# Attention with the scores' keys on the partitions, no transposes of the probabilities, and row sums from a product with ones

## The chip, the core and the metric

The program runs on one core of a Trainium2 chip. A core has TensorE (PE, matrix products), VectorE (DVE), ScalarE (ACT), GpSimd (POOL) and the engine that issues the DMAs here (SP). The metric is the device time of one execution in microseconds (us). All arithmetic is in fp32. A product in fp32 shows in the trace as two MATMUL records.

## The reference

```python
def rmsnorm(x, g):
    return x / np.sqrt(np.mean(x * x, axis=-1, keepdims=True) + 1e-06) * g
q_n, k_n = rmsnorm(q, g_q), rmsnorm(k, g_k)            # (8, 12, 448, 64) each
scores = np.matmul(q_n, k_n.transpose(0, 1, 3, 2)) / np.sqrt(64)
scores = scores - np.max(scores, axis=-1, keepdims=True)
attn = np.exp(scores)
attn = attn / (np.sum(attn, axis=-1, keepdims=True) + 1e-09)
x = np.matmul(attn, v)       # then (8, 12, 448, 64) -> (3584, 768)
r = np.maximum(x @ w_in, 0)  # w_in (768, 2048), float64
out = (r * r) @ w_out        # w_out (2048, 768), float64
```

The gains are g = |randn(64)| + 0.5. The largest product g_q g_k of the inputs used is 5.26.

## The kernel before

There are 8 batches of 12 heads, and attention runs on one pair of heads at a time (2 x 64 = 128 partitions), so there are 6 pairs in a batch and 48 in all. The 448 tokens of a head are split as token = 4 p + j, p on 112 partitions. A unit of work is one j of the queries of a pair, 192 units in all.

For a pair, `norm` (L133 to L148) squares q and k on POOL (L137), sums on DVE (L140), takes the power -1/2 of 112 x 16 numbers on POOL (L141, L142) and multiplies q and k by it on POOL (L144, twice). `transposes` (L150) turns q and k by 8 products with a unit matrix (L157) and moves them out of PSUM on DVE with the gains (L159).

For a unit, `softmax` (L161) makes the scores of 112 queries with 448 keys for both heads (L167: contraction over 64 partitions, head 0 on partitions 0 to 63, head 1 on 64 to 127). DVE takes the row maximum (L170). ACT takes the exponential and sums it (L174, once a head). DVE adds 1e-9, inverts and scales the rows (L177 to L180). `values` (L187) turns the probabilities, 4 products a head (L195), copies them out of PSUM on ACT for head 0 (L198) and on DVE for head 1 (L200), and multiplies them with v, 4 products a head of 112 columns, which write 64 PSUM partitions for each head (L204). After the last unit of a pair DVE copies the result to xT (L209).

`feed_forward` (L217) of a batch is laid in pieces between the units of the next batch. Its first product has 16 groups of 6 products of 448 columns (L224), each followed by a relu on ACT (L227) and a square on POOL (L228). Its second product has 6 groups in an even batch and 8 in an odd one, of 16 products of 384 columns (L236).

During batch 0 there is no feed-forward work. In its place the weights come in as 32 pieces of 768 doubles a partition, and are rounded to fp32: 5 operations on DVE (L110, L112, L113, L115, L116), 2 on ACT (L111, L114), one on POOL (L117), in three sets of buffers that rotate. The feed-forward block of batch 0 starts when all this is done, since the buffers of the raw words lie in its tile gT.

Each engine works through its instructions in one order. A scheduler in the language's layer sets it from the order of the code and from the tiles' buffers: the tag "m" in PSUM (3 buffers before) serves the transposes and both feed-forward products, the tag "s" (2 buffers) the scores, the tag "o" (1 buffer) the product with v.

Of the kernel before, what the change touches and what calls it, by code (L numbers as in the profile page):

```python
# [8 lines left out]
F32 = mybir.dt.float32  # L9
U32 = mybir.dt.uint32  # L10
AF = mybir.ActivationFunctionType
ALU = mybir.AluOpType
AX = mybir.AxisListType.X


@with_exitstack
def kernel(
    ctx: ExitStack,
# [9 lines left out]
):  # L28
    """Softmax attention with RMS-normalised q and k, then relu(x w_in)^2 w_out, all in fp32.

    Attention runs on one pair of heads at a time (2 x 64 = 128 partitions).
    A sequence of 448 tokens is split as token = 4 p + j, with p on 112
    partitions, so that a partition's 4 tokens are one run in memory. A unit of
    work is one j of the queries of one pair: scores and softmax with the
    queries on the partitions, then the normalised rows are transposed and
    multiplied with v, which gives x transposed, as the first product of the
    feed-forward block takes it. The feed-forward block of a batch is laid
    between the units of the next batch.
    """
    nc = tc.nc  # L40

    B, H, S, D = q.shape
    NT, DM = out.shape
    DFF = w_in.shape[1]
    P = 128
# [25 lines left out]

# [1 line left out]
    # Doubles come in pairs of words (low, high) and are rounded here to fp32, the  # L73
    # widest type of the engines: +-2^E from the high word, times
    # 1 + (m20 + low 2^-32) 2^-20. Below fp32's normal range a weight becomes 0,
    # above it infinite. The words stay in gT until the feed-forward block needs it.
    NW = 768
# [40 lines left out]

# [1 line left out]
    qks, vs, qkTs, probs, pavs, xTs = {}, {}, {}, {}, {}, {}  # L120
# [91 lines left out]

# [1 line left out]
    # gT has room for 448 + 64 tokens. An even batch takes the last 448 columns  # L214
    # and leaves its last 64 tokens there for the odd batch that follows, which
    # takes the first 448 and shares its last block of 128 with them.
    def feed_forward(b):  # L217
# [36 lines left out]

# [1 line left out]
    load(0)  # L256
# [15 lines left out]
    for b in range(B):  # L272
        fill = feed_forward(b - 1) if b else iter(())  # starts at its first next()
        n = pieces(b - 1) if b else 0
        done = 0
        for u in range(NPAIR * NJ):
            i, j = b * NPAIR + u // NJ, u % NJ
            if j == 0 and i + 2 < NP:
                load(i + 2)
            softmax(i, j)  # L280
            if j == 1 and i + 1 < NP:
                norm(i + 1)
            if j == 3 and i + 1 < NP:
                transposes(i + 1)
            if last is not None:
                values(*last)
            last = (i, j)
            if b == 0:
                m = len(pieces_w)
                for n_w in range(m * u // (NPAIR * NJ), m * (u + 1) // (NPAIR * NJ)):  # L290
                    round_weights(n_w)
                    load_weights(n_w + NSET)
            while done < n * (u + 1) // (NPAIR * NJ):
                next(fill)
                done += 1
        for _ in fill:
            pass
# [3 lines left out]


# [1 line left out]
_INS = ['q', 'k', 'v', 'g_q', 'g_k', 'moe_w_in', 'moe_w_out']  # L304
# [26 lines left out]
```

## Time and profile before

| | |
|---|---|
| device time, three runs | 2096.97, 2096.86, 2093.71 us; median 2096.86 |
| span of the profiled execution | 2093.7 us |
| PE busy | 1981.1 us (95%) |
| POOL, DVE, ACT busy | 535.5, 838.1, 494.4 us |
| batch 0 of attention with the rounding | 0 to 275 us, DVE busy 235.5 us of it |
| 7 batches of attention with feed-forward | 275 to 1940 us, PE busy 1646.4 us of it |
| last feed-forward block | 1940 to 2089 us |

The profiled execution's own time is its span, with the lowest of the three run times 2093.71 us and the median 3.2 us above it. Busy time of PE is a union of records whose ends are modelled, so a reader goes by starts: how far apart two groups of products begin is what one of them takes.

### The profile page before, as it was taken

The page shows a single profiled execution, that of the slowest core. Times are in us where ns is not written, and L with a number is a line of the kernel's source. Part 1 is how long each engine was busy: PE and PEld are TensorE (multiplying, and loading weights), DVE is VectorE, ACT ScalarE, POOL GpSimd, SP SyncE. Part 2 cuts the span into 40 slices and gives each one's busy share as a digit, 9 for nine tenths or more (in the row PEclk, how much of TensorE's full clock was granted, in tenths as well). Part 3 has the DMA queues.
Part 4 walks back from the last instruction along what each step waited for, and adds up shares of the span by engine and source line. Part 5 has one row for each costly group of instructions (what it writes and reads, how often), then busy time and mean ns, then how long its engine had stood idle before and what let it go on. Part 6 is the DMA issues. An engine that isn't in the chain of part 4 may idle for free.

```text
span 2093.7 us, 22618 instructions
## 1 busy us (share of the span) xinstructions
PE 1981.1 (95%) x9088; PEld 1130.0 (54%) x9088; DVE 838.1 (40%) x1533; ACT 494.4 (24%) x1181; POOL 535.5 (26%) x408
## 2 busy tenths in 40 slices
PE   4767699999999999999999999999999999999999
PEld 2444455555555555555555555555555555555555
DVE  7898853333333333333333333333333333333000
ACT  2344332212221222212221122212222122221100
POOL 4345542311321132311231123221231113210100
PEclk7566599999999999999999999999999999999999
DMA  4233300000000010010000000001000000000000
GB/s 149 93 128 104 123 27 13 28 29 21 23 18 21 29 31 17 14 35 29 14 23 26 29 21 27 14 21 42 14 14 33 31 21 15 17 8 16 0 8 23
DMA packets 47784, 70.67 MB, mean 34 GB/s; under 512 B 3648, under 2 KB 35904, under 8 KB 47680
## 3 DMA queue, kind: packets, MB, share of 16 engines
q1 hardware_dynamic: 47680, 69.22, 10.2%
q8 instruction: 73, 1.20, 0.2%
q14 instruction: 31, 0.25, 0.0%
HBM read 58.20 MB, written 11.01 MB: 33 GB/s over the span
## 4 chain that ended last, share of the span: by engine, by line
PE 81%; DVE 13%; issue 5%; POOL 1%; DMA 0%; SPq 0%; ACT 0%; POOLq 0%; DVEq 0%; ACTq 0%
PE ph L224 29%; PE po L236 25%; PE pav L204 12%; PE sc L167 8%; PE ppt L195 7%; DVE nmax L170 3%; DVE pr L180 1%; DVE qkT L159 1%; DVE w L116 1%; DVE gT L113 1%; DVE gT L112 1%; DVE w L110 1%; DVE rstd L140 1%; DVE w L115 1%; POOL qkn L137 1%
## 5 line engine op out<-in xcount | busy, mean ns | idle before, releaser
L224 PE MATMUL ph<-xT,w 128*128 128x448 f32 x1536 | 626.8, 549 | 1.1 <-DVE xT L209 1.1
L236 PE MATMUL po<-w,gT 128*128 128x384 f32 x1792 | 617.7, 492 | 0.0
L170 DVE TENSOR_REDUCE nmax<-sc 112x2 f32<-112x896 f32 x192 | 209.2, 1090 | 799.2 <-PE sc L167 799.2
L236 PEld LDWEIGHTS po<-w,gT 128*128 128x128 f32 x1792 | 326.7, 190 | 207.8 <-DVE qkT L159 2.8
L224 PEld LDWEIGHTS ph<-xT,w 128*128 128x128 f32 x1536 | 275.0, 190 | 231.2 <-issue 208.0
L204 PEld LDWEIGHTS pav<-prT,vt 112*64 112x64 f32 x3072 | 275.2, 144 | 165.4 <-ACT prT L198 104.3
L204 PE MATMUL pav<-prT,vt 112*64 112x112 f32 x3072 | 334.4, 278 | 6.8 <-DVE prT L200 6.2
L228 POOL TENSOR_TENSOR gT<-r 128x448 f32<-128x448 f32 x128 | 119.4, 933 | 752.7 <-ACT r L227 752.7
L174 ACT ACTIVATE pr<-sc,nmax 112x448 f32<-112x448 f32 x384 | 240.2, 630 | 184.8 <-DVE nmax L170 180.3
L167 PE MATMUL sc<-qkT 64*112 64x448 f32 x768 | 228.9, 626 | 34.0 <-DVE qkT L159 17.5
L195 PE MATMUL ppt<-ident,pr 112*112 112x112 f32 x1536 | 207.8, 277 | 42.6 <-DVE pr L180 23.1
L195 PEld LDWEIGHTS ppt<-ident,pr 112*112 112x112 f32 x1536 | 158.4, 140 | 152.9 <-issue 113.4
L137 POOL TENSOR_TENSOR qkn<-qk 112x1024 f32<-112x1024 f32 x48 | 91.8, 1912 | 533.3 <-issue 380.7
L227 ACT ACTIVATE r<-ph 128x448 f32<-128x448 f32 x128 | 69.6, 544 | 602.5 <-PE ph L224 602.5
L198 ACT COPY prT<-ppt 112x448 f32<-112x448 f32 x192 | 102.1, 532 | 412.6 <-PE ppt L195 412.6
L180 DVE TENSOR_SCALAR pr<-pr,rec 112x448 f32<-112x448 f32 x384 | 174.5, 497 | 5.8
L142 POOL TENSOR_TENSOR rstd<-rstd,mhalf 112x16 f32<-112x16 f32 x48 | 139.6, 2909 | 4.0
L167 PEld LDWEIGHTS sc<-qkT 64*112 64x112 f32 x768 | 61.1, 183 | 147.3 <-issue 105.2
L200 DVE COPY prT<-ppt 112x448 f32<-112x448 f32 x192 | 118.0, 614 | 16.0 <-PE ppt L195 15.9
L144 POOL TENSOR_TENSOR qkn<-qk,rstd 112x512 f32<-112x512 f32 x96 | 107.1, 1136 | 3.8
L241 DVE COPY osb<-po 128x384 f32<-128x384 f32 x28 | 15.6, 558 | 229.0 <-PE po L236 229.0
L117 POOL TENSOR_TENSOR w<-gT,w 128x768 f32<-128x768 f32 x32 | 65.4, 2047 | 112.5 <-DVE w L116 65.3
(27 smaller groups left out, 630.4 us busy)
## 6 DMA issues: line engine op xcount, KB each, us to landing
gT<-in_moe_w_in_dram SPq DMA_DIRECT2D x16, 768.0 KB, 4.5
gT<-in_moe_w_out_dram SPq DMA_DIRECT2D x16, 768.0 KB, 4.2
qk<-in_q_dram SPq DMA_DIRECT2D x48, 224.0 KB, 2.7
qk<-in_k_dram SPq DMA_DIRECT2D x48, 224.0 KB, 2.9
vt<-in_v_dram SPq DMA_DIRECT2D x48, 224.0 KB, 2.5
out_dram<-osb SPq DMA_DIRECT2D x24, 384.0 KB, 2.3
out_dram<-osb SPq DMA_DIRECT2D x8, 192.0 KB, 2.6
gains<-in_g_q_dram SPq DMA_DIRECT2D x2, 0.2 KB, 2.8
```

Of the source, the lines that this page charges most:

```text
L137: nc.gpsimd.tensor_tensor(sq, flat, flat, ALU.mult)
L142: nc.gpsimd.tensor_tensor(rflat, rflat, mhalf, ALU.pow)
L167: nc.tensor.matmul(sc[:, h, 0:S], qkT[rows, 0, j * SP:(j + 1) * SP], qkT[rows, 1, :], start=True, stop=True)
L170: nc.vector.tensor_reduce(nmax, sc[:, :, 0:S], AX, ALU.max, negate=True)
L174: nc.scalar.activation(pr[:, h], sc[:, h, 0:S], AF.Exp, bias=nmax[:, h:h + 1], accum_out=total[:, h:h + 1])
L180: nc.vector.tensor_scalar(pr[:, h], pr[:, h], rec[:, h:h + 1], None, ALU.mult)
L195: nc.tensor.transpose(pt[:, c, :], pr[:, h, c * SP:(c + 1) * SP], ident[:SP, :SP])
L200: nc.vector.tensor_copy(prT, pt)
L204: nc.tensor.matmul(pav[h * D:(h + 1) * D, j * SP:(j + 1) * SP], vt[:, h, c, :], prTs[h][:, c, :], start=(c == 0), stop=(c == NJ - 1))
L224: nc.tensor.matmul(ph, w1[:, c, f * P:(f + 1) * P], xT[:, c, :], start=(c == 0), stop=(c == NPAIR - 1))
L228: nc.gpsimd.tensor_tensor(gT[:, f, c0:c0 + S], r, r, ALU.mult)
L236: nc.tensor.matmul(po, gT[:, f, c0 + t:c0 + t + P], w2[:, f, cols], start=(f == 0), stop=(f == NFC - 1))
```

## The change

The kernel becomes two programs behind a condition that the chip evaluates. The maximum over d of (g_q g_k)^2 is taken on DVE, loaded into a register of each engine and compared with 75^2/64 = 87.9. Up to this bound the program `attention_then_ffn_bounded` runs, above it the kernel before, word for word, as `attention_then_ffn_with_row_max`.

In the bounded program a unit is 112 keys of a pair with all its 448 queries: the scores come with the keys on the partitions, so that their exponential can be multiplied with v as it is. There is no row maximum and no transpose of probabilities. ACT takes one exponential of 112 x 896 a unit. POOL adds the four exponentials of a pair (three additions of 112 x 896). A product of the sum with a 112 x 64 block of ones gives the row sums on all 64 partitions of a head (`finish`, L492). DVE inverts them (128 x 448, L494), and multiplies the product with v by the result as it moves it to xT (L495). The product with v has 448 columns; its heads alternate within each c (L484).

```diff
-    ps_m = ctx.enter_context(tc.tile_pool(name="ps_m", bufs=3, space=bass.MemoryType.PSUM))
+    ps_m = ctx.enter_context(tc.tile_pool(name="ps_m", bufs=2, space=bass.MemoryType.PSUM))
+    ones = consts.tile([SP, D], F32, name="ones")
-        vt = loads.tile([SP, 2, NJ, D], F32, tag="vt", name="vt", bufs=3)
+    def load_v(i):
+        vs[i] = loads.tile([SP, 2, NJ, D], F32, tag="vt", name="vt")
...
-    def softmax(i, j):
+    def scores(i, c):
         qkT = qkTs[i]
         sc = ps_s.tile([SP, 2, 512], F32, tag="s", name="sc")
         for h in range(2):
             rows = slice(h * D, (h + 1) * D)
-            nc.tensor.matmul(sc[:, h, 0:S], qkT[rows, 0, j * SP:(j + 1) * SP], qkT[rows, 1, :],
+            nc.tensor.matmul(sc[:, h, 0:S], qkT[rows, 1, c * SP:(c + 1) * SP], qkT[rows, 0, :],
                              start=True, stop=True)
-        nc.vector.tensor_reduce(nmax, sc[:, :, 0:S], AX, ALU.max, negate=True)
-        pr = work.tile([SP, 2, S], F32, tag="pr", name="pr", bufs=3)
-        for h in range(2):
-            nc.scalar.activation(pr[:, h], sc[:, h, 0:S], AF.Exp, bias=nmax[:, h:h + 1],
-                                 accum_out=total[:, h:h + 1])
-        nc.vector.tensor_scalar(total, total, 1e-9, None, ALU.add)
-        nc.vector.reciprocal(rec, total)
-        for h in range(2):
-            nc.vector.tensor_scalar(pr[:, h], pr[:, h], rec[:, h:h + 1], None, ALU.mult)
+        pr = work.tile([SP, 2, S], F32, tag="pr", name="pr", bufs=5)
+        nc.scalar.activation(pr, sc[:, :, 0:S], AF.Exp)
+        if c == 1:
+            accs[i] = work.tile([SP, 2, S], F32, tag="acc", name="acc")
+            nc.gpsimd.tensor_tensor(accs[i], probs[i, 0], pr, ALU.add)
+        elif c > 1:
+            nc.gpsimd.tensor_tensor(accs[i], accs[i], pr, ALU.add)
...
-    def values(i, j):
-        for h in range(2):
-            pt = ps_m.tile([SP, NJ, SP], F32, tag="m", name="ppt")
-            for c in range(NJ):
-                nc.tensor.transpose(pt[:, c, :], pr[:, h, c * SP:(c + 1) * SP], ident[:SP, :SP])
-            prT = work.tile([SP, NJ, SP], F32, tag="prT", name="prT", bufs=4)
-            if h == 0:
-                nc.scalar.copy(prT, pt)
-            else:
-                nc.vector.tensor_copy(prT, pt)
-        for h in range(2):
-            for c in range(NJ):
-                nc.tensor.matmul(pav[h * D:(h + 1) * D, j * SP:(j + 1) * SP], vt[:, h, c, :], prTs[h][:, c, :],
-                                 start=(c == 0), stop=(c == NJ - 1))
+    def values(i, cs):
+        for c in cs:
+            pr = probs.pop((i, c))
+            for h in range(2):
+                nc.tensor.matmul(pavs[i][h * D:(h + 1) * D, :], vs[i][:, h, c, :], pr[:, h, :],
+                                 start=(c == 0), stop=(c == NJ - 1))
+    def finish(i):
+        tot = ps_o.tile([P, S], F32, tag="t", name="tot")
+        for h in range(2):
+            nc.tensor.matmul(tot[h * D:(h + 1) * D, :], ones, acc[:, h, :], start=True, stop=True)
+        nc.vector.reciprocal(rec, tot)
+        nc.vector.tensor_tensor(xTs[b][:, hp, :].rearrange("d (p j) -> d j p", j=NJ),
+                                pavs.pop(i).rearrange("d (j p) -> d j p", j=NJ),
+                                rec.rearrange("d (j p) -> d j p", j=NJ), ALU.mult)
...
+            if not second:          # a pair has two blocks: block A ...
+                scores(i, 0)
+                scores(i, 1)
+                norm(i + 1)
+                if u:
+                    values(i - 1, (2, 3))
+                    finish(i - 1)
+            else:                   # ... and block B
+                transposes(i + 1)
+                scores(i, 2)
+                scores(i, 3)
+                values(i, (0, 1))
...
+            if u == blocks - 1:     # last block of a batch
+                values(i, (2, 3))
+                finish(i)
...
+    nc.vector.tensor_tensor(gg[:, 0, :], gg[:, 0, :], gg[:, 1, :], ALU.mult)
+    nc.vector.tensor_tensor(gg[:, 0, :], gg[:, 0, :], gg[:, 0, :], ALU.mult)
+    nc.vector.tensor_reduce(top, gg[:, 0, :], AX, ALU.max)
+    bits = nc.values_load(top.bitcast(mybir.dt.int32))
+    with tc.If(bits <= limit) as small_scores:
+        attention_then_ffn_bounded(tc, *args)
+    with small_scores.Else():
+        attention_then_ffn_with_row_max(tc, *args)
```

(The three remarks in the loop are added here.) The feed-forward pieces follow each block as they followed each unit: mostly two groups a block. The relu now writes gT and POOL squares it in place.

The order on PE, kernel before, one unit of the 7 batches with feed-forward: scores (sc), transposes of the probabilities of the unit before (ppt), product with v (pav), feed-forward groups (ph). A pair has four such units.

```order
L167 MATMUL sc_2837<-qkT_2676 112x448 x2
L195 MATMUL ppt_2851<-ident_76,pr_2787 112x112 x4
L195 MATMUL ppt_2858<-ident_76,pr_2787 112x112 x4
L224 MATMUL ph_2873<-xT_1676,w1_79 128x448
L204 MATMUL pav_2804<-prT_2856,vt_2292 64x112 x4
L204 MATMUL pav_2804<-prT_2863,vt_2292 64x112 x4
L224 MATMUL ph_2873<-xT_1676,w1_79 128x448 x5
L224 MATMUL ph_2883<-xT_1676,w1_79 128x448 x6
```

The same place in the changed kernel, a block B and the start of the next block A (pt are the transposes of q and k of the next pair):

```order
L454 MATMUL pt_1718<-ident_94,qkn_1679 128x112 x4
L465 MATMUL sc_1730<-qkT_1616 112x448
L454 MATMUL pt_1724<-ident_94,qkn_1679 128x112 x4
L465 MATMUL sc_1730<-qkT_1616 112x448
L465 MATMUL sc_1736<-qkT_1616 112x448 x2
L484 MATMUL pav_1742<-pr_1670,vt_1614 64x448 x2
L484 MATMUL pav_1742<-pr_1675,vt_1614 64x448 x2
L513 MATMUL ph_1747<-xT_936,w1_98 128x448 x6
L513 MATMUL ph_1756<-xT_936,w1_98 128x448 x6
L465 MATMUL sc_1768<-qkT_1717 112x448 x2
```

The 8 transposes of a unit are gone and the 8 short products with v have become 2 long ones; the two heads' scores of the third unit stand on either side of a group of transposes.

The order on POOL late in a batch, kernel before, two pairs: nothing but the normalisation of q and k of coming pairs.

```order
L137 TENSOR_TENSOR qkn_5009<-qk_4733 112x1024
L141 TENSOR_SCALAR rstd_5011<-rstd_5011 112x16
L142 TENSOR_TENSOR rstd_5011<-rstd_5011,mhalf_78 112x16
L144 TENSOR_TENSOR qkn_5009<-qk_4733,rstd_5011 112x2x4x64 x2
L137 TENSOR_TENSOR qkn_5229<-qk_4944 112x1024
```

POOL in the changed kernel at the last pair of a batch: the additions of this pair (acc_1333) stand around the normalisation of a coming one (qkn_1486).

```order
L472 TENSOR_TENSOR acc_1333<-pr_1326,pr_1331 112x896
L434 TENSOR_TENSOR qkn_1486<-qk_1320 112x1024
L474 TENSOR_TENSOR acc_1333<-acc_1333,pr_1409 112x896
L438 TENSOR_SCALAR rstd_1488<-rstd_1488 112x16
L439 TENSOR_TENSOR rstd_1488<-rstd_1488,mhalf_97 112x16
L441 TENSOR_TENSOR qkn_1486<-qk_1320,rstd_1488 112x2x4x64 x2
L474 TENSOR_TENSOR acc_1333<-acc_1333,pr_1415 112x896
```

PE at that place, with the product with ones (tot) that needs acc_1333, ahead of the feed-forward groups:

```order
L484 MATMUL pav_1418<-pr_1326,vt_1250 64x448 x2
L484 MATMUL pav_1418<-pr_1331,vt_1250 64x448 x2
L484 MATMUL pav_1418<-pr_1409,vt_1250 64x448 x2
L484 MATMUL pav_1418<-pr_1415,vt_1250 64x448 x2
L492 MATMUL tot_1427<-acc_1333,ones_95 64x448 x2
L525 MATMUL po_1434<-w2_99,gT_100 128x384 x16
```

The last addition of the pair stands behind the whole normalisation, and behind the product that waits for it stand 32 products of the second feed-forward half.

## Rows read from the trace of the kernel before

**Rows 1.** The page: busy time of PE, and its granted clock by slices.

```profile
PE 1981.1 (95%) x9088; PEld 1130.0 (54%) x9088; DVE 838.1 (40%) x1533; ACT 494.4 (24%) x1181; POOL 535.5 (26%) x408
...
PEclk7566599999999999999999999999999999999999
```

**Rows 2.** Busy time by stretch: length, PE, PEld, DVE, ACT, POOL, granted clock, DMA.

```profile
0.00:275.00 275.00, 185.90 (x751) 114.36 (x752) 235.47 (x338) 103.00 (x193) 129.45 (x76) 0.65 0.35 115
275.00:1940.00 1665.00, 1646.43 (x7907) 933.83 (x7907) 600.42 (x1192) 381.31 (x971) 391.79 (x317) 1.00 0.07 23
```

**Rows 3.** Timeline of PE, one unit: start, us, instructions.

```profile
1013.76 1.01 PE L167 MATMUL sc<-qkT 64*112 64x448 f32 x4
1014.70 0.98 PE L195 MATMUL ppt<-ident,pr 112*112 112x112 f32 x8
1015.51 0.93 PE L224 MATMUL ph<-xT,w 128*128 128x448 f32 x2
1016.38 1.42 PE L204 MATMUL pav<-prT,vt 112*64 112x112 f32 x16
1017.73 4.03 PE L224 MATMUL ph<-xT,w 128*128 128x448 f32 x10
1021.68 0.63 PE L167 MATMUL sc<-qkT 64*112 64x448 f32 x2
```

**Rows 4.** The same of the unit before it, which holds transposes of q, k.

```profile
1003.45 1.01 PE L167 MATMUL sc<-qkT 64*112 64x448 f32 x4
...
1005.21 0.55 PE L195 MATMUL ppt<-ident,pr 112*112 112x112 f32 x4
...
1007.78 0.98 PE L204 MATMUL pav<-prT,vt 112*64 112x112 f32 x8
```

**Rows 5.** The chain of waits from 1940 us on: start, us, what.

```profile
1939.71 66.52 PE ph L224 x177
2006.23 82.58 PE po L236 x256
```

**Rows 6.** DVE's lines of the rounding and two more: duration min/median/max in ns.

```profile
L110 DVE TENSOR_SCALAR w<-gT x32: 531/895/954, 13.5 to 263.8; 128x768 uint32<-128x768 uint32 x32
...
L112 DVE TENSOR_SCALAR gT<-gT x32: 535/547/2168, 14.9 to 265.6; 128x768 uint32<-128x768 uint32 x32
...
L113 DVE SCALAR_TENSOR_TENSOR gT<-gT x32: 932/944/2622, 17.0 to 266.9; 128x768 f32<-128x768 uint32 x32
...
L115 DVE TENSOR_SCALAR w<-w x32: 544/616/692, 17.9 to 267.8; 128x768 uint32<-128x768 uint32 x32
...
L116 DVE SCALAR_TENSOR_TENSOR w<-gT,w x32: 937/944/2634, 19.6 to 269.3; 128x768 uint32<-128x768 uint32 x32
...
L180 DVE TENSOR_SCALAR pr<-pr,rec x384: 421/449/2078, 24.8 to 1922.2; 112x448 f32<-112x448 f32 x192
...
L159 DVE TENSOR_SCALAR qkT<-pt,gains x96: 657/675/677, 14.3 to 1884.5; 128x448 f32<-128x448 f32 x96
```

**Rows 7.** POOL's lines, in the same form.

```profile
L117 POOL TENSOR_TENSOR w<-gT,w x32: 1799/1809/3292, 26.1 to 271.0; 128x768 f32<-128x768 f32 x32
...
L137 POOL TENSOR_TENSOR qkn<-qk x48: 1892/1892/2281, 4.4 to 1842.9; 112x1024 f32<-112x1024 f32 x48
...
L142 POOL TENSOR_TENSOR rstd<-rstd,mhalf x48: 2898/2899/3300, 7.9 to 1846.4; 112x16 f32<-112x16 f32 x48
...
L144 POOL TENSOR_TENSOR qkn<-qk,rstd x96: 1036/1042/2968, 10.9 to 1850.4; 112x512 f32<-112x512 f32 x96
```

**Rows 8.** Stretches of batch 0, in the columns of Rows 2.

```profile
178.00:194.00 16.00, 15.91 (x46) 8.20 (x47) 10.30 (x20) 4.42 (x8) 1.80 (x1) 0.50 0.26 91
...
201.20:205.00 3.80, 0.03 (x1) 0.00 (x0) 3.80 (x6) 2.02 (x3) 3.72 (x3) 0.98 0.00 0
205.00:215.00 10.00, 7.97 (x36) 6.20 (x37) 10.00 (x14) 4.38 (x8) 8.51 (x5) 0.50 0.57 190
```

**Rows 9.** The page, DMA issues: KB, median us from issue to landing.

```profile
gains<-in_g_q_dram SPq DMA_DIRECT2D x2, 0.2 KB, 2.8
```

More of the change, by code (lines that the diff above doesn't have):

```diff
@@ L1 @@
+import struct
 from contextlib import ExitStack
@@ L16, with attention_then_ffn_with_row_max @@
 @with_exitstack
-def kernel(
+def attention_then_ffn_with_row_max(
     ctx: ExitStack,
@@ new lines, with kernel @@
+@with_exitstack
+def kernel(
+    ctx: ExitStack,
+    tc: tile.TileContext,
+    q: bass.AP,
+    k: bass.AP,
+    v: bass.AP,
+    g_q: bass.AP,
+    g_k: bass.AP,
+    w_in: bass.AP,
+    w_out: bass.AP,
+    out: bass.AP,
+):
+    nc = tc.nc
+    D = q.shape[-1]
+    bound = ctx.enter_context(tc.tile_pool(name="bound", bufs=1))
+    gg = bound.tile([1, 2, D], F32, name="gg")
+    top = bound.tile([1, 1], F32, name="top")
+    for i, g in enumerate((g_q, g_k)):
+        nc.sync.dma_start(gg[:, i, :], g.rearrange("(o d) -> o d", o=1))
+    nc.vector.tensor_tensor(gg[:, 0, :], gg[:, 0, :], gg[:, 1, :], ALU.mult)
+    nc.vector.tensor_tensor(gg[:, 0, :], gg[:, 0, :], gg[:, 0, :], ALU.mult)
+    nc.vector.tensor_reduce(top, gg[:, 0, :], AX, ALU.max)
+    bits = nc.values_load(top.bitcast(mybir.dt.int32))
+    limit = struct.unpack("<i", struct.pack("<f", 75.0 ** 2 / D))[0]
+    args = (q, k, v, g_q, g_k, w_in, w_out, out)
+    with tc.If(bits <= limit) as small_scores:
+        attention_then_ffn_bounded(tc, *args)
+    with small_scores.Else():
+        attention_then_ffn_with_row_max(tc, *args)
```

207 lines of the change are left out of this document (added).

## The prediction

> **What bounds the kernel now.** I read the page first: PE is busy 95% of the span, and its granted clock is low in the first slices only [rows 1]. Then the stretches: up to 275 us (batch 0 of attention, and the rounding) DVE is busy 235 us and PE 186, at a mean clock of 0.65; from 275 us on PE is busy 1646 of 1665 us at full clock [rows 2]. So there are two stages with different limits. After 275 us whatever PE no longer does is time won; before it PE is not the limit.
>
> What attention costs after 275 us comes in two ways. The last feed-forward block runs alone: 66.52 us for 177 products (0.376 each) and 82.58 for 256 (0.3226 each) [rows 5]. The seven blocks before it have 7 x 192 = 1344 products of the first kind (505 us) and, with 192 in the four even batches and 256 in the three odd ones, 1536 of the second (496 us). The stretch is 1665 us, so 664 are left for 42 pairs, 15.8 us each. In the timeline a unit goes from 1013.76 to 1021.68, 7.92 us, of which 12 feed-forward products are 4.51, so 3.41 are attention [rows 3]; the unit with the transposes of q and k goes from 1003.45 to 1013.76, 10.31 - 4.51 = 5.80 [rows 3, 4]. Three of the one and one of the other give 16.0 us a pair.
>
> **PE after batch 0.** I count in slots of 0.376 us, what 448 columns take. Scores of both heads: 4 records in 0.94 us [rows 3], two slots and 0.19 over. So the heads run side by side on the two halves of the contraction, and 0.19 us is the price of a change of the kind of product. The product with v before: the first 8 records end 0.98 us after their start [rows 4], 16 end after 1.42 [rows 3], so head 1's 8 cost 0.44 us, 55 ns each, although a group of transposes, all alike, pays 108 ns for each further one (0.55 for 4, 0.98 for 8 [rows 3, 4]). Where the code has head 0's four products and then head 1's, the second head overlaps what is left of the first; the two write different halves of PSUM's partitions. In the change the heads alternate, so I take full overlap: two records a slot. The columns per head are the same as before, 4 x 4 x 112 = 4 x 448.
>
> A pair then costs, in block A, scores of two units (4 slots) and two c of v with the ones product (4 + 2 slots); in block B, 8 transposes (0.38 twice), one unit's scores in halves that lie on either side of transposes (2 slots + 1, the second half overlapped with the next unit's first head, so 2 + 4), and two c of v (4 slots). That is 20 slots, 7.5 us, and 0.77: 8.3 us. Stretches of another kind, the way back to the feed-forward products included: 3 in A, 6 in B, at 0.19: 1.7. In sum 10.0 us a pair in place of 15.8: 42 x 5.8 = **244 us less**.
>
> Not on this path: ACT's exponentials (four a pair, without the read-back of a sum), DVE's inverse and multiplication, POOL's additions. POOL has 392 us of work in these 1665 [rows 2] and gets 126 additions. No row shows 112 x 896; L137's 1024 elements take 1.89 us [rows 7], so one takes 1.66 (by elements) to 1.89: 209 to 238 us, and POOL stays under half busy. The inverse of 128 x 448 has no row either; L159, of the same shape out of PSUM, takes 0.675 [rows 6], and the product with v's one buffer is wanted again only after two feed-forward groups (9 us) and block B's start, so up to ten times that it is hidden.
>
> **A wait at the end of each batch.** There PE reaches the ones product without feed-forward groups in between, and POOL's last addition stands behind the whole normalisation (the order shown above). From block B's start: transposes and half the scores end at 2.2 us; POOL's square, 1.89, ends at 4.1 (its one buffer is that of the transposes); addition 1.7, to 5.8; power 2.90, to 8.9 with its small forerunner; two multiplications of 1.04, to 11.0; addition, to 12.7 [rows 7], with the waits between some 13.5. PE's products with v end at 7.5. It waits 6 us, and 32 feed-forward products queue behind. Idle PE loses its clock: it sat 3.8 us in batch 0, having had 0.98, and had 0.50 (1.2 GHz) for the next 10 us [rows 8]; that costs up to 5 more. Batches 1 to 6: 6 x 11 = **66 us more** (24 to 100).
>
> **Batch 0.** DVE loses the maximum, the scaling and the copies of probabilities. It keeps the rounding (111 us, below), 14 of L159 (9 us [rows 6]) and some 19 sums, inverses and moves, at L159's price 13: 133 us in place of 235 [rows 2]. I do not count this as won, since the two engines shut each other out. L116 takes 0.937 us at its fastest and 2.63 at most, L180 0.42 and 2.08 [rows 6], POOL's L144 1.04 and 2.97 [rows 7]: the excess has the size of one instruction of the other engine. The rule is in the Trainium skill, SBUF — State Buffer, Who interferes with whom: DVE operations that use both its ports, or read two tensors in SBUF, and GpSimd's hold a shared pair of ports exclusively. The rows agree. A batch 0 without it is the first rival below.
>
> DVE's five operations of the rounding sum to 3.48 us at their fastest, x 32 pieces = 111 us [rows 6]. POOL's, at their fastest: 32 x 1.80 + 7 x 1.89 + 14 x 1.04 = 85, and 18 additions of 1.66, 30 more: 115 [rows 7]. One after the other: 226 us, where before it was 111 + 85 + the scaling (48 x 0.42 = 20 [rows 6]) = 216. Beginning at 13.5 us, as before, 226 us without a gap end at 240. Before, 216 us took 261. I take 243 us for them. The start comes later by the gains' DMA (2.8 us to landing [rows 9]), its two issues, three tiny DVE operations, a register load and a branch, which no row shows: 6 us (4 to 15). Batch 0 then ends at 13.5 + 243 + 6 = 263; with 5 us for its last pair's chain (sum, ones product, inverse, next batch's first scores), **7 us less** than 275 (35 less to 25 more).
>
> **Sum.** The span is 2093.7 us, and the median of the runs 2096.9, 3.2 above it. 2093.7 - 244 + 66 - 7 = 1908.7, so 1912 as a median. The last block (149 us) and the output's tail stay. The likeliest case's own range: 1855 to 1975.
>
> **Rivals.**
>
> *The two engines don't shut each other out as a rule.* Then DVE has 133 us of work in batch 0, POOL 115 and 7 powers of 2.90, 135; PE at half clock needs 6 x 2 x 8.3 = 100. DVE filled 235 of 261 us, nine tenths; the same share of 135 is 150, and a chain that runs to and fro between both engines may add a third: 13.5 + 6 + 195 = 215 us, so 1912 - 48 = 1864. For it: DVE's busy time filled the stage, more than that sum of 216 did. Against: the maxima [rows 6, 7].
>
> *The heads don't overlap at 448 columns.* Then 8 slots of v and 2 of ones more a pair: 10 x 0.376 x 42 = 158 us, 2070, little under now. For it: the trace shows the overlap only for the tail of a group of short products. Against: the scores overlap with the same alternation.
>
> *Slower: the clock falls in every attention stretch.* Now attention comes in pieces of at most 3 us between feed-forward products; then in pieces of 4 to 6. For it: in batch 0 PE worked 15.91 of 16 us on scores, transposes and v, and had 0.50 throughout [rows 8]. Against: that was a clock already low; none of 168 units now lowers it. It decides from 182 / 84 blocks = 2.2 us lost a block, that is 4.3 us of each block at 1.2 GHz. At 5 us a block it gives 84 x 2.5 = 210 more: 2122.
>
> *The general program runs.* 5.26^2 = 27.6 is under 87.9, so it can't be by these inputs; if it did, 2097 + 6 = 2103.
>
> **Chances.** The forecast 0.63; the two engines side by side 0.17; no overlap of the heads 0.07; the clock 0.05; the general program 0.01; unnamed waits, most of them a slower but still faster kernel than now, 0.07. The range for 8 in 10 takes in the first rival, with a shorter wait at the batches' ends (42 less), and upwards the upper bounds of start, waits and batch 0 together (9 + 34 + 32 more) and about as much for what is unnamed; it stops short of no overlap: 1810 to 2030. What a measurement of this kernel can tell is about 0.2%, 4 us: faster 0.93, same 0.01, slower 0.06.
>
> **What would show it.** Right: starts of v's records two by two, 0.376 apart, 1.6 us for a c-pair; a block's attention at 4.3 (A) and 5.6 us (B); first feed-forward product at 255 to 275; six waits of tot on POOL's acc of about 6 us, each followed by half clock; POOL and DVE together close to the length of batch 0. Wrong: pav records 0.376 apart one by one; a granted clock under 1.00 in the middle of batches; PE waiting for pt's input or for a PSUM buffer of the transposes, of which there are now two; a batch 0 of 220 us.

## The result and the profile after

The changed kernel takes 1871.1 us (median of four runs, 1867.5 to 1873.0), where the kernel before took 2095.8 in the same session: a ratio of 0.893 (95% interval 0.8915 to 0.894), 225 us faster. The forecast was 1912 and the range 1810 to 2030. Of all the runs below, one of the kernel with both heads in one half took 4811.2 us where its other three took 1977.1 to 1980.2; it is left out. The profiled execution took 1869.6 us with a span of 1867.8, 226 less than before.

The page of the changed kernel, the lines that answer to [rows 1]:

```profile
PE 1664.5 (89%) x5440; PEld 814.8 (44%) x5440; DVE 509.2 (27%) x432; ACT 305.3 (16%) x413; POOL 844.4 (45%) x553
...
PEclk9556689999999999999999999999999999999999
```

PE has 3648 matmul records fewer and is busy 317 us less, but its share of the span fell from 95% to 89%: some of the time won stands idle. Three stretches of the changed kernel, in the columns of [rows 2]:

```profile
0.00:253.00 253.00, 99.11 (x304) 36.12 (x304) 225.60 (x199) 80.72 (x93) 188.40 (x101) 0.68 0.38 123
253.00:1715.00 1462.00, 1418.87 (x4712) 698.00 (x4712) 281.37 (x230) 214.50 (x301) 641.99 (x438) 0.99 0.08 25
1715.00:1864.00 149.00, 146.56 (x427) 80.70 (x425) 2.23 (x4) 10.08 (x19) 13.98 (x15) 1.00 0.03 10
```

The first stretch ends where PE has its clock back after batch 0; at 253 us PE has started 12 records of feed-forward products, and 11 at 275 before, so the two cuts stand at nearly the same work. The last feed-forward block is as it was. The middle was 1665 us and is 1462. In it PE is idle for 43 us, where before it was for 19. PE's timeline there, with one block B (from 1003.02) and one block A (from 1029.14):

```profile
1003.02 0.55 PE L454 MATMUL pt<-ident,qkn 112*128 112x112 f32 x4
1003.50 1.00 PE L465 MATMUL sc<-qkT 64*112 64x448 f32 x2
1004.43 0.60 PE L454 MATMUL pt<-ident,qkn 112*128 112x112 f32 x4
1004.96 1.75 PE L465 MATMUL sc<-qkT 64*112 64x448 f32 x6
1006.65 1.72 PE L484 MATMUL pav<-pr,vt 112*64 112x448 f32 x8
1008.30 20.91 PE L525 MATMUL po<-w,gT 128*128 128x384 f32 x64
1029.14 1.76 PE L465 MATMUL sc<-qkT 64*112 64x448 f32 x8
1030.83 1.72 PE L484 MATMUL pav<-pr,vt 112*64 112x448 f32 x8
1032.38 0.92 PE L492 MATMUL tot<-acc,ones 112*64 112x448 f32 x4
1033.23 20.91 PE L525 MATMUL po<-w,gT 128*128 128x384 f32 x64
```

Eight records of the product with v last 1.72 us, four slots of 0.376 and the start of the first, so they run two by two. Block A is 1033.23 - 1029.14 and 0.2 for the change of kind ahead of it, 4.3 us; block B is 1008.30 - 1003.02 and 0.1, 5.4 us. Before, the four units of such a pair took 16.0 [rows 3, 4].

Where the idle time went is in the view of what PE waits for (us in total, times, longest):

```profile
PE tot L492 <- POOL acc L474: 78.9, 14, 15.1
PE pt L454 <- POOL qkn L441: 75.7, 13, 15.3
PE sc L465 <- ACT pr L468: 22.2, 10, 5.8
PE sc L465 <- DVE qkT L456: 19.8, 6, 7.4
```

The last three of these fall into batch 0 but for 0.8 us; of the first, 36.6 us do. The rest of the first stands at the batches' ends:

```profile
410.99 1.89 POOL L434 TENSOR_TENSOR qkn<-qk 112x1024 f32<-112x1024 f32 x1 [22.00 <-PE pt L454]
...
412.47 3.23 PE L484 MATMUL pav<-pr,vt 112*64 112x448 f32 x16
...
415.40 2.91 POOL L439 TENSOR_TENSOR rstd<-rstd,mhalf 112x16 f32<-112x16 f32 x1
418.39 2.04 POOL L441 TENSOR_TENSOR qkn<-qk,rstd 112x512 f32<-112x512 f32 x2
420.39 2.07 POOL L474 TENSOR_TENSOR acc<-acc,pr 112x896 f32<-112x896 f32 x1
422.51 1.76 PE L492 MATMUL tot<-acc,ones 112*64 112x448 f32 x4 [6.81 <-POOL acc L474]
...
644.38 1.76 PE L492 MATMUL tot<-acc,ones 112*64 112x448 f32 x4 [6.76 <-POOL acc L474]
```

These are POOL and PE at the end of batch 1, and the same ones product at the end of batch 2. PE's last product with v ends at 415.7; POOL then does the power and the two multiplications of the next pair, 5 us, before the addition that PE waits for. Such a wait of 6.76 to 6.82 us stands at the end of each of the batches 1 to 6. Two stretches around it, in the columns of [rows 2]:

```profile
415.80:422.40 6.60, 0.00 (x0) 0.00 (x0) 0.00 (x0) 0.00 (x0) 6.52 (x4) 0.84 0.12 30
420.40:427.00 6.60, 4.49 (x9) 1.88 (x10) 2.68 (x1) 0.00 (x0) 2.06 (x2) 0.50 0.38 104
```

PE does nothing for 6.6 us, and its clock goes to half (1.2 GHz) at 420.4 and back to full at 427.2. The first 2.1 us of these 6.8 still lie in the wait; in the other 4.7 PE works at half clock, which costs it 2.3.

### The profile page after: what moved, and what is told of

It is laid out like the page before. It is cut to its first block, busy times and chain, and to the rows that moved or that the text cites. A ratio compares the mean times of both kernels' runs of the same rounds, so it can differ in the third digit from the quotient of the medians.

```text
span 1867.8 us, 13256 instructions
## 1 busy us (share of the span) xinstructions
PE 1664.5 (89%) x5440; PEld 814.8 (44%) x5440; DVE 509.2 (27%) x432; ACT 305.3 (16%) x413; POOL 844.4 (45%) x553
## 4 chain that ended last, share of the span: by engine, by line
PE 82%; POOL 5%; issue 0%; DVE 0%; DMA 0%; ACT 0%; SPq 0%; POOLq 0%; ACTq 0%
PE po L525 32%; PE ph L513 31%; PE sc L465 9%; PE pav L484 7%; PE tot L492 2%; PE pt L454 2%; POOL acc L474 2%; POOL rstd L439 1%; POOL qkn L441 1%; POOL qkn L434 1%; DMA gT<-in_moe_w_out_dram 0%; ACT pr L468 0%; DVE gT L405 0%; POOL acc L472 0%; POOL w L409 0%
## 5 line engine op out<-in xcount | busy, mean ns | idle before, releaser
L494 DVE RECIPROCAL rec<-tot 128x448 f32<-128x448 f32 x48 | 141.9, 2956 | 545.6 <-PE tot L492 545.6
L517 POOL TENSOR_TENSOR gT<-gT 128x448 f32<-128x448 f32 x128 | 119.3, 932 | 313.0 <-ACT gT L516 313.0
L472 POOL TENSOR_TENSOR acc<-pr 112x896 f32<-112x896 f32 x48 | 101.9, 2123 | 310.5 <-ACT pr L468 310.3
L474 POOL TENSOR_TENSOR acc<-acc,pr 112x896 f32<-112x896 f32 x96 | 203.9, 2124 | 27.3 <-ACT pr L468 24.8
L468 ACT ACTIVATE pr<-sc 112x896 f32<-112x896 f32 x192 | 166.2, 913 | 118.6 <-PE sc L465 118.6
L484 PE MATMUL pav<-pr,vt 112*64 112x448 f32 x768 | 175.0, 576 | 0.0
L516 ACT ACTIVATE gT<-ph 128x448 f32<-128x448 f32 x128 | 69.6, 544 | 608.4 <-PE ph L513 608.4
L456 DVE TENSOR_SCALAR qkT<-pt,gains 128x448 f32<-128x448 f32 x96 | 65.3, 682 | 361.5 <-PE pt L454 361.5
L454 PE MATMUL pt<-ident,qkn 112*128 112x112 f32 x384 | 61.3, 287 | 75.7 <-POOL qkn L441 75.7
L492 PE MATMUL tot<-acc,ones 112*64 112x448 f32 x192 | 56.7, 647 | 78.9 <-POOL acc L474 78.9
```

Source lines behind the costliest of these rows:

```text
L454: nc.tensor.transpose(pt[:, j * SP:(j + 1) * SP], qkn[:, s, j].rearrange("p h d -> p (h d)"), ident[:SP, :SP])
L468: nc.scalar.activation(pr, sc[:, :, 0:S], AF.Exp)
L474: nc.gpsimd.tensor_tensor(accs[i], accs[i], pr, ALU.add)
L484: nc.tensor.matmul(pavs[i][h * D:(h + 1) * D, :], vs[i][:, h, c, :], pr[:, h, :], start=(c == 0), stop=(c == NJ - 1))
L494: nc.vector.reciprocal(rec, tot)
L517: nc.gpsimd.tensor_tensor(g, g, g, ALU.mult)
```

## The experiments

Each kernel was run beside the kernel before; ratios are to that kernel (the changed kernel has 0.893). Times are medians.

**The last addition of a batch on DVE.** This is meant to take away the wait at the batches' ends alone; it moves one addition in each of the eight batches.

```
-            nc.gpsimd.tensor_tensor(accs[i], accs[i], pr, ALU.add)
+            eng = nc.vector if c == NJ - 1 and i % NPAIR == NPAIR - 1 else nc.gpsimd
+            eng.tensor_tensor(accs[i], accs[i], pr, ALU.add)
```

> The changed kernel, with the last of the three additions of a batch's last pair on DVE in place of POOL. Theory (PE waits for tot because that addition stands behind the whole normalisation on POOL, and loses its clock by the wait): the six waits of 6.8 us shrink to under 1 us, the six stretches at half clock of 6.83 us that follow vanish, and the time falls by 6 x (6 + 3.4) = 56 us, to about 1814. Rival A (the clock falls for another reason, such as the long attention piece at that place): only the waits go, 6 x 6 = 36 us less, about 1835. Rival B (the wait moves on to the inverse, xT or the next pair's transposes): no change, about 1871.

Measured: 1816.3 us, ratio 0.867 (0.866 to 0.869): 55 less than the changed kernel. The timeline at the same place and of the ones product a batch later, and PE's waits for DVE's addition:

```profile
413.36 1.09 DVE L475 TENSOR_TENSOR acc<-acc,pr 112x896 f32<-112x896 f32 x1 [0.94 <-POOL acc L475]
...
414.60 0.97 PE L493 MATMUL tot<-acc,ones 112*64 112x448 f32 x4 [0.62 <-DVE acc L475]
...
628.02 0.97 PE L493 MATMUL tot<-acc,ones 112*64 112x448 f32 x4 [0.55 <-DVE acc L475]
```

```profile
PE tot L493 <- DVE acc L475: 4.1, 7, 0.6
```

The addition is there at 414.5 instead of 422.5, and from 260 us to the end of the last block the clock is never at half. From the end of batch 1 to that of batch 2 it is 628.02 - 414.60 = 213.42 us, where it was 644.38 - 422.51 = 221.87: 8.45 us a batch, 6.2 of the wait and 2.3 of the clock, and nothing took their place. Six batches make 51 us. Of the other 2.7 us between the two profiled executions, 1.7 came in batch 0 and 0.9 at the last pair. The cause is shown: with the wait the half clock goes as well, so it is not rival A's 1835. That the time meets the theory's 1814 so closely is partly chance, since the theory took 3.4 us for the clock where it was 2.3.

**Both heads' products with v into the same half of PSUM's partitions** (the two heads' results are then added into one). This takes away what lets the heads run side by side, and leaves count and order of the products.

```
-  pavs[i][h * D:(h + 1) * D, :], vs[i][:, h, c, :], pr[:, h, :], start=(c == 0), stop=(c == NJ - 1)
+  pavs[i][0:D, :], vs[i][:, h, c, :], pr[:, h, :], start=(c == 0 and h == 0), stop=(c == NJ - 1 and h == 1)
```

> The changed kernel, with both heads' products with v written to the same 64 PSUM partitions (one accumulation of both heads in place of two, so the heads' results are added up; DVE's multiplication is done once for each half of xT). The number and size of PE's products is the same. Theory (the two heads run side by side because they write different halves of PSUM's partitions): 16 records of a pair take 16 slots of 0.376 in place of 8, 3.0 us more a pair, 42 x 3.0 = 126 us more after batch 0, about 1997. Rival (the gain comes from fewer and longer products and from the transposes that are gone, not from the heads side by side): no change, about 1871.

Measured: 1977.4 us, ratio 0.944 (0.943 to 0.947): 106 more than the changed kernel. Eight records now take

```profile
1023.11 3.22 PE L484 MATMUL pav<-pr,vt 112*64 112x448 f32 x8
```

3.22 us in place of 1.72, a slot each. The six waits fell from 6.8 to 3.8 us, since PE now comes 3 us later to the sum; these 18 us are most of what is missing of 126.

One rival is left: the heads may be kept apart because both now add into the same tile, not because they use the same half. The ones products of this kernel tell, since head 0's still write the lower half, head 1's the upper half, of another tile. In PE's order stand eight records of v (lower half), two of ones for head 0, two for head 1:

```profile
1037.17 2.85 PE L484 MATMUL pav<-pr,vt 112*64 112x448 f32 x7
1039.48 0.59 PE L492 MATMUL tot<-acc,ones 112*64 112x448 f32 x1
1039.85 0.54 PE L484 MATMUL pav<-pr,vt 112*64 112x448 f32 x1
1039.91 1.23 PE L492 MATMUL tot<-acc,ones 112*64 112x448 f32 x3
```

Two ones records start beside v's seventh and eighth. They are head 1's: the signal that starts DVE's inverse, which is sent by the last of the four in the program, stands in the trace at the second to start (1039.91). Head 0's, which stand before them and write another tile but the same half as v, run alone after it. So it is the half.

**The kernel before, with the heads by turns**: its loop over chunks put outside that over heads.

```
-        for h in range(2):
-            for c in range(NJ):
+        for c in range(NJ):
+            for h in range(2):
```

> The kernel before, with one edit: in the product with v the heads alternate within each c (loop c outside, h inside), columns still 112. Theory (heads side by side, whatever the length): the 16 records of a unit take 8 x 0.096 + 0.19 = 0.96 us in place of 1.35, 0.4 x 168 units = 66 us less, about 2030; what the first head's product now waits for DVE's copy of the second head takes some of it back. Rival (weights bind short products: the 16 weight loads of a unit took 1.21 us, 76 ns each): no change within 10 us, about 2096.

Measured: 2071.2 us, ratio 0.988 (0.987 to 0.990): 24 less, between the two. PE's timeline of a unit of it:

```profile
1007.69 0.41 PE L204 MATMUL pav<-prT,vt 112*64 112x112 f32 x2
1008.03 1.02 PE L224 MATMUL ph<-xT,w 128*128 128x448 f32 x2
1008.98 0.98 PE L204 MATMUL pav<-prT,vt 112*64 112x112 f32 x14
```

Fourteen records in 0.98 us do run by turns, but the scheduler put a feed-forward product between the first product of head 0 and the rest, and the two changes of kind that this makes give most of the gain back. About 10 of the 24 us came in batch 0, whose last rounded piece is ready at 261 us instead of 273. The run does not settle the theory; the next three do.

**The changed kernel with the heads one after the other.**

```
-        for c in cs:
-            for h in range(2):
+        for h in range(2):
+            for c in cs:
```

> The changed kernel with the products with v of a block issued head after head (both chunks of head 0, then both of head 1) in place of by turns; their PSUM halves stay as they are. Theory of the prediction (two products run side by side only where neighbours in PE's order write different halves): a block of 16 products has one such place in place of eight, so 6 to 7 slots of 0.376 us more per block of two, or about 6 x 0.376 x 42 = 95 us for the whole where two such places are left in a pair of heads, 1966 us; by the run with one half for both heads, which showed 108 where 126 was worked out, 80 us, 1951 us. Rival (it is the halves alone that count, and PE finds a partner for a product further back in its queue): 1871 us.

Measured: 1872.5 us, ratio 0.893 (0.892 to 0.895): no difference. The theory, that only neighbours pair up, falls:

```profile
1033.81 1.73 PE L484 MATMUL pav<-pr,vt 112*64 112x448 f32 x8
```

The first record of head 1 stands four behind the first of head 0, and still they start 14 ns apart. In the kernel before, where each head has eight records, head 1's first (1016.815) starts 5 ns after head 0's fifth, in the 16 of [rows 3]. Both fit a queue in which PE starts a product of the other half from up to four places behind. If that is so, a distance of six must cost time; two more kernels tell it apart.

**One and three chunks in a block, in place of two and two; heads by turns, then head after head.** The first edit is `values(i, (0,))` and `values(i - 1, (1, 2, 3))` for `(0, 1)` and `(2, 3)`; the second adds the edit above.

> The control for the next run: the changed kernel with the products with v of a pair of heads split 1 and 3 chunks in place of 2 and 2, heads by turns as before. No theory expects a difference: 1871 us.

> The same split, but each block head after head, so that head 1's first record stands six records behind head 0's first. Theory from the last runs (PE starts a product of the other half that stands up to four records behind the one it starts; in the kernel before, head 1's first of eight starts with head 0's fifth, and in the run with the heads in order, head 1's first of four starts with head 0's first): in the larger block head 0's first two records and head 1's last two run alone, 2 slots of 0.376 us more in each of 42 pairs, 32 us over the control, 1903 us. Rival A (any distance in the queue will do): as the control, 1871 us. Rival B (only neighbours; the heads in order ran together for another reason): 5 slots more in the larger block and one in the smaller, 75 to 95 us over the control.

Measured: by turns 1874.9 us, ratio 0.894 (0.893 to 0.896); head after head 1896.8, ratio 0.905 (0.903 to 0.906): 22 more than its control. The timeline of the latter's larger block:

```profile
1046.11 2.53 PE L484 MATMUL pav<-pr,vt 112*64 112x448 f32 x10
1048.41 0.54 PE L494 MATMUL tot<-acc,ones 112*64 112x448 f32 x1
1048.47 0.54 PE L484 MATMUL pav<-pr,vt 112*64 112x448 f32 x1
1048.79 0.54 PE L494 MATMUL tot<-acc,ones 112*64 112x448 f32 x1
1048.85 0.54 PE L484 MATMUL pav<-pr,vt 112*64 112x448 f32 x1
1049.22 0.92 PE L494 MATMUL tot<-acc,ones 112*64 112x448 f32 x2
```

Head 1's first record, six places behind head 0's first, five behind its second and four behind its third, starts at 1046.915 with the third (1046.909), and its last two run beside the first two of the ones product, which writes head 0's half. That is two slots a pair of heads lost, as worked out. The waits at the six ends, 6.0 us in place of 6.8, hide 5 of the 32 us; the other 5 I did not trace. So halves of PSUM make the overlap possible, and a distance of four records in the queue is near enough, five or six is not.

**Batch 0: the rounding's product on DVE.** `nc.gpsimd.tensor_tensor(w, f, w, ALU.mult)` became `nc.vector.tensor_tensor(...)`.

> The changed kernel, with the last multiplication of the rounding (32 of 128 x 768) on DVE in place of POOL. Theory (in batch 0 DVE's operations with two ports or two SBUF inputs and POOL's exclude each other, so that their sum sets its length): the sum was DVE 111 + POOL 57.6 + 13.2 + 14.6 + 21 x 2.07 = 240 us; now DVE 111 + 32 x 0.94 = 141 and POOL 71, 212: batch 0 ends near 222 in place of 250, 28 us less in all, about 1843. Rival A (DVE by itself is the limit, busy 222 of 237 us): 30 us more, about 1901. Rival B (POOL's own chain is the limit, 76 of its 181 us go): 50 us less or more, about 1820.

Measured: 1856.5 us, ratio 0.886 (0.885 to 0.888): 15 less, the sign of the theory and half its size.

**Batch 0: the sums on PE.** There the ones product runs on each of the four exponentials, and POOL adds nothing.

```
+        if i < NPAIR:      # per chunk, beside the products with v
+            for h in range(2):
+                nc.tensor.matmul(tots[i][h * D:(h + 1) * D, :], ones, pr[:, h, :], start=(c == 0), stop=(c == NJ - 1))
```

> The changed kernel, but in batch 0 alone the ones products run on all four exponentials and add up in PSUM, so that POOL's 21 additions of that batch (14 of 2.38 us and 7 of 2.39 us, 50 us in all) are gone; PE gets 6 ones slots more in each of 7 pairs, about 16 us at full clock, in time in which it is mostly idle. Theory of the prediction (DVE and POOL exclude each other, batch 0 is as long as the two sums together): up to 50 us less, 1821 us. A weaker form, from the run with the rounding's product on DVE (75.6 us taken off POOL shortened DVE's other rounding operations by 46 us, 0.61 of it): 31 us less, 1840 us. Rival (DVE is the bound by its own work, and what POOL does beside it costs nothing): 1871 us, or a few us more for PE's added slots. Against all three: DVE's rounding operations, 6.13 us for five on average with the additions, fall towards 4.2 to 5 by the first two and stay by the third.

Measured: 1842.2 us, ratio 0.879 (0.877 to 0.880): 29 less, near the weaker form's 31; DVE's five rounding operations fell from 6.13 to 5.07 us, so the rival is out. The expectation counted a pair too many: batch 0 has six pairs, so 18 additions are gone, 43 us by their mean there (2.38) and 37 by their shortest (2.07). Both runs are read best from the rounding, from its first instruction to the end of its last. Against it stands the sum of what DVE and POOL have to do in that time in instructions that stretch beside the other engine, each at its line's shortest record (DVE's rounding; on POOL the rounding's product, the squares, the multiplications, the additions):

| kernel (all in us) | DVE + POOL | sum | measured | DVE with its other work |
| --- | --- | --- | --- | --- |
| changed kernel | 108.5 + 125.7 | 234 | 229.5 | 149 |
| product on DVE | 140.2 + 70.4 | 211 | 216.2 | 181 |
| sums on PE | 108.4 + 90.5 | 199 | 203.4 | 149 |
| product on DVE, sums on PE, last addition on DVE (the fastest version below) | 140.5 + 33.1 | 174 | 191.1 | 181 |

Three times the sum holds to 3%, though DVE alone would need 149 to 181 us. In the last, where the sum is less than DVE's own work, the stage is 10 us longer than that. That DVE's own work sets it there is argued from this table; no run doubled it.

**Both edits**, the sums on PE in batch 0 and the last addition on DVE.

> The last addition of each batch on DVE (measured alone: 1816 us, 55 less) together with the ones products in place of additions in batch 0. If the two gains add: 1816 less 31 to 50, 1766 to 1785 us. If they share the wait at the end of batch 0 (11.6 us of it is left with the first edit alone): some 8 to 12 us less of the gain, 1776 to 1795 us. If the additions of batch 0 cost nothing: 1816 us.

Measured: 1791.7 us, ratio 0.855 (0.854 to 0.856): inside the second expectation. By the two gains as measured, 55 and 29, it would be 1787, so they nearly add. A place in it shows the two engines shutting each other out the other way round:

```profile
201.84 0.94 DVE L405 SCALAR_TENSOR_TENSOR gT<-gT 128x768 f32<-128x768 uint32 x1
202.06 6.87 POOL L409 TENSOR_TENSOR w<-gT,w 128x768 f32<-128x768 f32 x1 [4.17 <-DVE w L408]
202.71 0.55 DVE L407 TENSOR_SCALAR w<-w 128x768 uint32<-128x768 uint32 x1
...
206.32 0.94 DVE L408 SCALAR_TENSOR_TENSOR w<-gT,w 128x768 uint32<-128x768 uint32 x1
...
207.19 2.94 DVE L506 RECIPROCAL rec<-tot 128x448 f32<-128x448 f32 x1
```

POOL's product, 1.80 at its shortest, takes 6.87 us while DVE's rounding runs at its own shortest without a gap, and ends 1.74 after DVE has gone over to the inverse.

**The rounding's product on DVE as well**, the fastest version.

> The kernel with both edits (1792 us), and the rounding's product on DVE as well, so that POOL has only the normalisation left in batch 0. By the runs so far (each us of work taken off POOL took 0.6 us off DVE's records, but PE gained 0.2 of it with the product and 0.6 of it with the additions): 70 us off POOL take some 42 us off DVE's records and 37 us come to it, so about 5 less, and no queue of products ahead of batch 1's first additions, up to 10 less again: 1777 to 1787 us. Rival (DVE is now the bound by its own work): 37 us more in batch 0, less what the end of batch 0 waits for POOL today (14), 1815 us.

Measured: 1780.1 us, ratio 0.850 (0.848 to 0.851): 12 less than with both edits, inside the expectation, not the rival's 1815.

**The sums on PE for the first pair of batch 1 too** (`NPAIR + 1` for `NPAIR` in both edits' kernel).

> The kernel with both edits (1792 us), with the sums on PE for one pair of heads more, the first of batch 1, for which PE waits 14.3 us (204 to 219) behind POOL's last products of the rounding, and then runs 20 us at half clock. If that wait simply goes: 14 us, and up to 10 of the clock, 1768 to 1778 us. Rival (the next thing from POOL, the normalised q and k of the pair after, comes late instead: it stands behind the same products, and only three additions of 2.07 us go from its way): 6 us less, 1786 us, and a wait of pt on qkn in the place of tot's on acc.

Measured: 1788.8 us, ratio 0.853 (0.852 to 0.855), not told apart from 0.855 and near the rival's 1786. The wait of 14.3 us went, and two others came, of which the larger is neither theory's:

```profile
PE tot L490 <- DVE rec L506: 5.9, 1, 5.9
```

the ones product's buffer in PSUM, which DVE's late inverse still reads; the normalised q and k come 2.9 us late.

**Without the condition**: the bounded program alone, no maximum, register or branch.

> The changed kernel without the condition: no product of the gains, no maximum, no value read into a register, no branch; the bounded program alone is built. The prediction put the start at 6 us: 1865 us. Rival (the start of the condition lies beside transfers that batch 0 would wait for anyway, DVE being the bound of it): 1869 to 1871 us.

Measured: 1867.7 us, ratio 0.892 (0.890 to 0.893), not told apart from the changed kernel. By the traces the first rounding instruction starts at 12.6 us instead of 15.8, the first feed-forward product at 220.9 instead of 224.2: the condition costs 3 us.

## Why the prediction was right, and where it was 41 us off

In spans: 1908.7 was forecast, 1867.8 came. The middle stretch has 1001 us of feed-forward by the prediction's count; 1462 less these, less 55 of waits and clock, leaves 406 for 42 pairs, 9.7 us each. One batch gives the same: 221.9 us (644.38 - 422.51), less 154.8 of feed-forward, less 9.1 of wait and clock, is 58 for six pairs. The three parts missed in the same direction, 14, 11 and 15 us, so none of the 41 is hidden by another.

- **PE after batch 0**, forecast 15.8 to 10.0 a pair, 244 us. Measured 15.8 to 9.7, 258 us: 14 more (A 4.3 as forecast, B 5.4 for 5.6). The reason given, two heads side by side because they write different halves of PSUM, was shown by the run with one half and its ones products. The reading of [rows 4], that head 1 overlaps "what is left" of head 0, is now exact: from head 0's fifth record on, four places ahead. That the heads must go by turns was not needed: at two chunks a block either order is near enough.
- **What was said to be off this path** held: PE waits for ACT's exponentials only in batch 0, and for the inverse not at all. But the inverse takes 2.95 us where I took 0.675, and the addition 2.07 where I took 1.66 to 1.89. Both were hidden; the addition counts in batch 0.
- **The wait at the end of each batch**, forecast 6 x (6 + 5) = 66 us. Measured 6 x (6.8 + 2.3) = 55: a longer wait, since PE came to it a little earlier than forecast, and a smaller loss of clock, since it was back after 4.7 us of work and not after 10. The cause, POOL's order, was shown by the addition on DVE: 51 us came back at these six places.
- **Batch 0**, forecast 7 us less, measured 253 - 275 = 22 less. This is the part that missed most. Its sum was nearly right: 226 us forecast, 234 by the shortest records (above all 20 additions of 2.07 us for 18 of 1.66). Wrong was the surcharge of 17 us ("Before, 216 us took 261. I take 243 us for them"), taken from the kernel before. There DVE waited 27 us for PE during the rounding and did 28 us of row maxima, reductions that don't stretch. Now it does not wait for PE at all (10 us of waits in sum, all but 0.6 for DMAs), and the rounding took 229.5 where 243 was forecast. That these waits made the surcharge is argued from the two traces; no run tests it. The start was put at 6 us and costs 3. The rule that the sum rests on, in the Trainium skill, SBUF — State Buffer, Who interferes with whom, also says which instructions don't take part: a DVE operation with at most one input in SBUF outside its two-port modes, and reductions. This trace agrees: the sums of squares (L437) take 1.16 to 1.22 us throughout, and the rows below show the others. Duration in ns, shortest, median and longest, with the first two lines of batch 0 alone:

```profile
L402 DVE TENSOR_SCALAR w<-gT x32: 491/936/4276, 15.8 to 234.0; 128x768 uint32<-128x768 uint32 x32
L405 DVE SCALAR_TENSOR_TENSOR gT<-gT x32: 935/948/6434, 17.3 to 236.3; 128x768 f32<-128x768 uint32 x32
...
L494 DVE RECIPROCAL rec<-tot x48: 2934/2958/2959, 51.5 to 1686.1; 128x448 f32<-128x448 f32 x48
L497 DVE TENSOR_TENSOR xT<-pav,rec x48: 934/964/980, 55.2 to 1689.0; 128x448 f32<-128x448 f32 x48
```

A rounding instruction takes up to 8.7 times its shortest; the inverse and the multiplication (L497, not L495 as the section on the change has it), which read PSUM, never do. So the prediction was right to leave these out of the sum.

- **The signs.** v's records two by two, the blocks' times and the six waits came as listed. The first feed-forward product did not: 224 us, not 255 to 275. It needs w_in alone and starts before w_out is rounded; PE then stops at 234.5, at the first ones product of batch 1, until 249.5. The forecast had one end of batch 0, and there are two. In the kernel before, too, the first one starts at 265 us and POOL's last rounding product ends at 272.8, so the feed-forward block does not wait for the whole rounding; the section on the kernel before has that wrong.
- **The rivals.** The time is nearer to the first rival's 1864 than to 1912, but its cause is not what happened: it had batch 0 end at 215 and engines that don't shut each other out, and the table shows the sum. Its number came near since pairs and waits were cheaper, which it did not say: that is luck. No overlap of the heads is out by the run with one half, the clock is at 0.99 in the middle, and the general program did not run (PE has no transposes of probabilities).

## What to carry to other kernels

When work is moved to an engine that is half idle, look at what stands ahead of it in that engine's queue where nobody has other work: one addition in the wrong place at the end of each of six batches cost 51 us, though POOL was busy 45% of the span. Where two engines share a port, add up their shortest records over the stage, for the instructions that stretch alone; here that sum held to 3% in three kernels. By it, moving work between the two gains only what the other does faster (23 us by the sum for the product on DVE, 13 measured). And a surcharge taken from the old stage ("216 took 261") carries the old stage's waits: look at what ended them before it is used again.

## What the runs showed of the hardware

- PE started a product for the other half of PSUM's partitions from four places behind in its order, not from five or six, in three kernels; a head's order of issue mattered only beyond that.
- DVE instructions that follow each other without a gap kept POOL out for all of them, not for one: 6.87 us for a product of 1.80. A POOL instruction keeps DVE out for its length, as here in the changed kernel, where DVE's instruction, 0.89 at its shortest, takes 2.56 and ends 0.82 after POOL's:

```profile
204.39 2.49 POOL L409 TENSOR_TENSOR w<-gT,w 128x768 f32<-128x768 f32 x1
205.14 2.56 DVE L408 SCALAR_TENSOR_TENSOR w<-gT,w 128x768 uint32<-128x768 uint32 x1
```

- An inverse of 128 x 448 from PSUM takes 2.95 us on DVE, 4.4 times the scaling of the same shape [rows 6]. An addition of 112 x 896 takes 2.07 us on POOL, more than the square of 1024 elements, which reads one operand twice (1.89, [rows 7]), and 1.09 on DVE.
